# Products of the output half tiles in pairs, and weight half tiles returned inside the second chain

## The chip, the cores and the metric

The kernel runs on one core of a Trainium2 chip. The core has TensorE (PE, with its weight load PEld), VectorE (DVE), ScalarE (ACT), GpSimd (POOL) and SyncE (SP); transfers between the memory (HBM) and the on-chip memory (SBUF) run on 16 DMA engines that all queues share. The metric is the time of one execution in device microseconds, the median of several runs.

## What is computed

Forward and backward of one decoding step of a transformer block, for 2 sequences (B = 2), one new position, 32 heads (64 pairs of sequence and head, called heads below), 8192 cached positions of width 128, all in bf16:

```python
mod = silu(c) @ w_mod                       # sa, ca, ga, sb, cb, gb
h = layernorm(x) * (1 + ca) + sa
scores = einsum('bhqd,bhkd->bhqk', h @ wq, k_cache) * Dh ** -0.5
o = einsum('bhqk,bhkd->bhqd', softmax(scores), v_cache)
x = x + ga * (o @ wo)
h = layernorm(x) * (1 + cb) + sb
out = x + gb * ((silu(h @ w1) * (h @ w3)) @ w2)
# outputs: out, and the gradients of x, k_cache, v_cache, wq, wo, w1, w3, w2, c, w_mod
```

The caches and their gradients hold nearly all of the bytes: per head 2 MB of K and 2 MB of V are read, and 2 MB of dK and 2 MB of dV are written. With the softmax weights p and ds the two gradients are outer products: dV = p (outer) d_o, dK = ds (outer) q.

## The kernel before

**Slots.** The program is written out by a list of events. `at(slot, place, f)` puts a step f into a numbered slot; within a slot the place decides (transposes first, then scores, products for the attention `PL_TT`, returns of buffers `PL_FREE`, products for dK `PL_DK`, single tasks `PL_TASK` last). The loop at the end (L1511 and on) goes through the slots and calls the steps. So each engine gets its instructions in exactly this order and works through them in order, waiting at each for what it needs. A slot has no fixed time.

**The two kinds of head.** An A head (`job_a`) reads K and V: 8 slots of transposes and scores (`a_t`, `a_s`), the softmax, the scaling of K on VectorE (`a_scale`), and products with V (`a_m`). A C head (L1219 and on) reads V again and makes dV and dK: 8 slots of transposes and scores from its slot s (`c_t`, `c_s`), then `c_ds`, and the outer products `c_dv` and `c_dk`. Its transposes are copied out of PSUM by ScalarE or, for two groups of eight in certain stages, VectorE (L383, L385).

**Stages.** Slots 0 to 312: A heads alone, every 8 slots. Slots 312 to about 700: A and C heads take turns, so that each kind comes every 16 slots (the interleaved stage). Slots 704 to 776: C heads alone, every 8 slots, beside them the second of the two chains. From slot 784: C heads alone every 8 slots, with the gradients of the weights put between them, until the last head, number 61, starts at slot 1016.

**The chains.** `steps_chain(b)` (L819) computes for one sequence all that follows the attention: output projection, layernorm, the gated products with w1, w3 and w2, and back. The first runs in the interleaved stage's beginning (slots 272 to 312), the second from slot 721 to 777 (`t1`). Within it, p5 is the last user of w2, p6 follows it; `turn_steps` are the last users of w1 and w3; `end_steps` holds q1, sums and q3.

**Half tiles.** Everything large goes through one pool of 21 buffers of 1 MB, `halfp`: half of a head's K or V, half of a dK or dV, a quarter of wo, pieces of w_mod and wq. w2 takes one, w1 and w3 take three. A count in the program, `free["half"]`, follows them: `release(n)` adds, and `pump` issues the next load of the sorted list `loads` on SP's queue while the count is above `keep` (2 in the interleaved stage, rising from 2 to 8 between slots 785 and 825):

```python
    def pump():
        while loads and free["half"] - keep[0] >= 1:
            loads.pop(0)[2]()
```

The count only sets the order. In the run each load or product into a buffer waits for the buffer's last user: for PE's reading of a K or V tile, or for the landing of an output that was written from it. SP's queue works in order too.

**Products.** `outer` (L1184) makes a quarter of a head's dV or dK (16 of 64 blocks, 128 x 2048) with one VectorE instruction (L1191). The first quarter of each half opens a half tile; after the second an output of 1 MB is issued on POOL's queue (L1196), and the buffer is counted as free six slots later (`back`). c_dv(n, q) is at slot s + 2q. c_dk(n, q) is at s + 11 + 2q, or s + 12 + 2q for the heads in `crow`, nearly all. `c_ds` comes one slot before the first c_dk.

**End of the second chain.** `chain_done` (L1480) at slot t1 drops the weight tiles, counts 4 + 4 half tiles as free (w2 and the three of w1 and w3; four of wo), and takes two for rows of the weight gradients.

Of the kernel before, what the change touches and what calls it, by code (L numbers as in the profile page):

```python
# [17 lines left out]
def kernel(  # L18
# [28 lines left out]
    B, Sq, D = A_x.shape  # L47
    assert Sq == 1 and B == 2
    _, H, Sk, Dh = A_k_cache.shape
# [13 lines left out]
    NG = KK // GRP  # L63
    NQ = KK // QK
    LAG = 2
# [3 lines left out]
    def fsz(fc):  # L69
        return P if fc < FC - 1 else FL  # L70
# [257 lines left out]
    def at(slot, place, f):  # L328
        seq[0] += 1
        events.setdefault(slot, []).append((place, seq[0], f))  # L330

    now = [0]
    PL_EXP, PL_T, PL_X, PL_S, PL_B, PL_MAX, PL_TT, PL_M, PL_FREE, PL_EV, PL_DS, PL_DK, PL_TASK = range(13)
# [8 lines left out]
# [4 lines that stand above are left out]
    def release(n=1):  # L346
        free["half"] += n
# [8 lines left out]
    def scr(n):  # L356
        if cur_ps[0] is None or now[0] - cur_ps[1] > 7:
            head_ps()
        if cur_ps[2] + n > 256:
            cur_ps[2] = 0  # L360
        o = 256 + cur_ps[2]
        cur_ps[2] += n
        return cur_ps[0][:, o:o + n]
# [235 lines left out]
    WH = HN // D  # L599
# [12 lines left out]
    wn = {}  # L612
# [29 lines left out]
    def w2_of(fc):  # L642
        t = wn["w2"][:, fc, :] if fc < WH else w2l[:, fc - WH, :]
        return t[:fsz(fc)]

    def rows_done():
        wn.pop("rows")
        release()
        pump()
# [41 lines left out]
    def small(n, nm, b):  # L691
        return tmp.tile([P, n], F32, name=nm, tag=nm)
# [124 lines left out]
    def steps_chain(b):  # L817
        out = []

        def put(n, f):  # L820
            out.append((n, f))
# [125 lines left out]
            nc.vector.tensor_mul(d_gate_bf[:, :, b], dg[:], dslg[:, :, b])  # L947

        put(1, p6)
        if b == 0:  # L950
            dot_steps(put)
        else:
            turn_steps(put)
# [3 lines left out]
    def dot_steps(put):  # L957
        def rows(v, vec, c0):
            n = min(4, FC - c0)
            ps = tps.tile([P, 4 * P], F32, name="rows", tag="tp")  # L960
            w = 0
            for k in range(n):
                r = fsz(c0 + k)
                nc.tensor.matmul(ps[:, k * P:k * P + r], vec[:r, c0 + k, 0:1].to_broadcast((r, P)),
                                 identb[:r, :r], start=True, stop=True)
                w = k * P + r
            if "rows" not in wn:
                wn["rows"] = hflat()[:]
                free["half"] -= 1
            nc.scalar.copy(wn["rows"][:, v * ROWV + c0 * P:v * ROWV + c0 * P + w], ps[:, 0:w])  # L970

        def one(v, nm, kc, hi):
            w = wn[(nm, hi)][:, kc, :]
            n = w.shape[-1]
            o = v * ROWV + hi * PW
            junk = ktp.tile([P, GRP * P], BF16, name="junkb", tag="kt")
            nc.vector.scalar_tensor_tensor(junk[:, 0:n], w, 1.0, wn["rows"][:, o:o + n], ALU.mult, ALU.mult,
                                           accum_out=dacc[:, kc, 2 * v + hi:2 * v + hi + 1])

        pairs = list(enumerate((("w3", d_up_bf), ("w1", d_gate_bf))))  # L980
        for v, (nm, vec) in pairs:
            for c0 in range(0, FC, 4):
                put(1, lambda v=v, vec=vec, c0=c0: rows(v, vec, c0))
        for v, (nm, vec) in pairs:
            for kc in range(NC):
                put(2, lambda v=v, nm=nm, kc=kc: one(v, nm, kc, 0))
                put(1, lambda v=v, nm=nm, kc=kc: one(v, nm, kc, 1))

    def turn_steps(put):
        b = B - 1  # L990
        groups = []
        for nm, vec in (("w3", d_up_bf), ("w1", d_gate_bf)):
            for f0 in range(0, FC, 2):
                fcs = [f for f in (f0, f0 + 1) if f < FC]
                def mm(kt, vec=vec, fcs=fcs):
                    ps = scr(NC)
                    for dc in range(NC):
                        for n, f in enumerate(fcs):
                            r = fsz(f)
                            nc.tensor.matmul(ps[:, dc:dc + 1], kt[:r, n * NC + dc, :], vec[:r, f, b:b + 1],  # L1000
                                             start=(n == 0), stop=(n == len(fcs) - 1))
                    return ps
                groups.append((nm, fcs, mm))

        def dacc_done(k, ps):
            nc.vector.tensor_copy(dacc[:, :, k], ps)

        turned_steps(put, [(lambda nm=nm, fcs=fcs: [w13_of(nm, kc, f)
                                                    for f in fcs for kc in range(NC)], mm)
                           for nm, fcs, mm in groups], dacc_done)  # L1010

    def end_steps(put, out, b, hold):
        nd = 4 if b == 0 else dacc.shape[-1]

        def sums():
            hold["ps"] = scr(2 * NC)
            nc.tensor.matmul(hold["ps"], onesf[:], hold["both"][:].rearrange("p t k -> p (t k)"),
                             start=True, stop=True)

        def q1():  # L1020
            nc.vector.tensor_reduce(d_h2[:, :, b], dacc[:, :, 0:nd], AX.X, ALU.add)
            both = tmp.tile([P, 2, NC], F32, name="both2", tag="both2", bufs=2)
            nc.vector.scalar_tensor_tensor(both[:, 0, :], mod[:, 4 * NC:5 * NC, b], 1.0, d_h2[:, :, b],
                                           ALU.add, ALU.mult)
            nc.vector.tensor_mul(both[:, 1, :], both[:, 0, :], xn2[:, :, b])
            hold["both"] = both

        def q3():
            st = small(2, "lnst", b)
            nc.vector.tensor_reduce(st[:], hold["ps"].rearrange("p (t k) -> p t k", t=2), AX.X, ALU.add)  # L1030
            nc.vector.tensor_scalar(st[:], st[:], 1.0 / D, None, ALU.mult)
            u = small(NC, "lnu", b)
            nc.vector.tensor_scalar(u[:], xn2[:, :, b], st[:, 1:2], st[:, 0:1], ALU.mult, ALU.add)
            nc.vector.tensor_sub(u[:], hold["both"][:, 0, :], u[:])
            nc.vector.scalar_tensor_tensor(d_x1[:, :, b], u[:], rstd2[:, 0, b:b + 1], dy_col[:, :, b],
                                           ALU.mult, ALU.add)
            nc.vector.tensor_mul(d_attn_bf[:, :, b], mod[:, 2 * NC:3 * NC, b], d_x1[:, :, b])

        put(0, q1)
        put(1, lambda: None)  # L1040
        put(0, sums)
        put(1, q3)
        return out
# [22 lines left out]
    sC = []  # L1066
    s = NG * H
# [10 lines left out]
    s = max(s, TC)  # L1078
# [12 lines left out]
    s = max(s, t1 + 5)  # L1091
# [55 lines left out]
    crow = {n for n in range(NHD) if R0 < sC[n] < A_END - NG or t1 < sC[n]}  # L1147
# [6 lines left out]
    def c_rows(n):  # L1154
        kts[("crow", n)] = rows_out(("c", n))
# [5 lines left out]
    def c_s(n, g):  # L1161
        if n in crow:
            return s_rows(("c", n), n, g, c_bank)
        b, h = hb(n)
        kt = kts.pop(("c", n, g))
        for j in range(GRP):
            cc = g * GRP + j
            nc.tensor.matmul(DP[n][:, cc:cc + 1], kt[:, j, :], DO_bf[:, b, h:h + 1], start=True, stop=True)  # L1168
# [36 lines left out]
    def c_dv(n, q):  # L1205
        outer(dvt, out_3, n, 1, E2[("c", n)], q)
        if q == NQ - 1:
            QD.pop((n, 1))
# [7 lines left out]
    def c_dk(n, q):  # L1216
        outer(dkt, out_2, n, 0, ds2[n], q)
        if q == NQ - 1:
            ds2.pop(n)  # L1219
            QD.pop((n, 0))  # L1220

    for n in range(NHD):
        s = sC[n]
        for g in range(NG):
            at(s + g, PL_T, lambda n=n, g=g: c_t(n, g))
            at(s + g + LAG, PL_S, lambda n=n, g=g: c_s(n, g))
        at(s - 3, PL_B, lambda n=n: c_spread(n))
        for q in range(NQ):
            at(s + 2 * q, PL_TT, lambda n=n, q=q: c_dv(n, q))
            at(s + NG + LAG + 1 + (n in crow) + 2 * q, PL_DK, lambda n=n, q=q: c_dk(n, q))  # L1230
        x = 1 if n in crow else 0
        if x:
            at(s + NG + LAG, PL_EXP, lambda n=n: c_rows(n))
            at(s + NG + LAG + 1, PL_EXP, lambda n=n: c_cols(n))
        at(s + NG + LAG + x, PL_DS, lambda n=n: c_ds(n))

        for hf in range(2):
            if n not in kept:
                want(s + hf * HG, lambda n=n, hf=hf: load_v(("c", n), n, hf))
# [240 lines left out]
    def chain_done():  # L1480
        wn.clear()
        wo_v.clear()
        release(4 + H // WH)
        for k in range(2):
            rowst[k] = hflat()
            free["half"] -= 1
        pump()

    at(t1, PL_TASK, chain_done)

    def more_keep():
# [52 lines left out]
```

## Time and profile before

| | |
|---|---|
| median of 3 runs | 1730.04 us (1729.28 to 1733.95) |
| the profiled execution's own time | 1731.2 us |
| its span | 1729.4 us |
| granted PE clock, mean | 0.83 |
| read from and written to HBM | 421.57 MB, 284.20 MB |
| outputs of 1 MB from half tiles | 256, median 17.9 us from issue to landing |
| loads of V halves | 252, median 14.3 us |
| loads of K halves | 128, median 19.6 us |

The span is that of the instructions on the core; the run's own time is measured around it. Busy times of engines are sums over the whole span. "DMA" is the mean busy share of the 16 DMA engines; packets of one engine overlap a little in the records, so a full stretch reads 1.01. The windows quoted below have, for each stretch, its length, the busy time and the number of instructions of PE, PEld, VectorE, ScalarE and GpSimd, the PE clock, the DMA share and GB/s. A line of waits has: who waited, for whom, the sum in us, how often, and the longest. A line of the timeline has start, length, engine, line and operation, and in brackets the idle time before it and what ended it.

### The profile page before, as it was taken

What the parts mean: (1) busy time and instruction counts of PE and PEld (TensorE: products, weight loads), DVE (VectorE), ACT (ScalarE), POOL (GpSimd) and SP (SyncE); (2) the same over time, 40 slices, a digit from 0 to 9 for tenths busy, and PEclk for the clock granted to TensorE, in tenths of its full rate; (3) what the DMA queues carried; (4) which work ended last, traced back from release to release, by engine and by line L of the source; (5) the groups of instructions that cost most, each with busy time, mean ns of one, the idle gap of its engine ahead of it and who ended that gap; (6) DMA issues with size and microseconds to landing.
All of it is one profiled execution on the core that took longest, in us unless ns stands there. A gap on an engine that the chain in (4) does not pass through costs nothing.

```text
span 1729.4 us, 48571 instructions
## 1 busy us (share of the span) xinstructions
PE 1447.8 (84%) x20883; PEld 1155.6 (67%) x20883; DVE 1149.6 (66%) x1575; ACT 1046.1 (60%) x1536; POOL 344.9 (20%) x726
## 2 busy tenths in 40 slices
PE   5999999989988878887788888975599997797962
PEld 5999998879776666665666666875355565455551
DVE  2666666867877677666667766785586675666554
ACT  4666666646565556555555555697576676566772
POOL 0333333322211111111111112111121111111111
PEclk7999999988999898898888998698765567556586
DMA  9999999999999999999999998999999999999997
GB/s 382 418 418 419 418 419 388 419 387 390 379 412 424 425 425 420 424 418 418 420 419 418 424 419 358 397 416 420 426 411 419 413 410 419 423 420 420 417 420 303
DMA packets 109379, 708.92 MB, mean 410 GB/s; under 512 B 11175, under 2 KB 17683, under 8 KB 27243
## 3 DMA queue, kind: packets, MB, share of 16 engines
q1 hardware_dynamic: 67280, 421.59, 59.4%
q0 software_dynamic: 36864, 268.45, 37.4%
q10 hardware_dynamic: 5019, 15.78, 2.3%
q8 instruction: 163, 2.67, 0.6%
q14 instruction: 53, 0.43, 0.1%
HBM read 421.57 MB, written 284.20 MB: 408 GB/s over the span
## 4 chain that ended last, share of the span: by engine, by line
DMA 45%; PE 35%; DVE 6%; ACT 6%; issue 5%; SPq 1%; POOL 0%; ACTq 0%; POOLq 0%; DVEq 0%
DMA out_dram<-half 24%; DMA half<-in_A_k_cache_dram 16%; PE tp L380 14%; PE m_ps L483 8%; DVE half L1191 4%; DMA out_dram<-stg 3%; ACT kt L385 3%; PE s_ps L442 2%; PE k_ps L505 2%; PE s_ps L433 2%; PE m_ps L413 1%; DMA half<-in_w_mod_dram 1%; PE m_ps L1323 1%; DVE ek L468 1%; PE k_ps L413 1%
## 5 line engine op out<-in xcount | busy, mean ns | idle before, releaser
L385 ACT COPY kt<-tp 128x1024 bf16<-128x1024 bf16 x794 | 796.6, 1017 | 560.0 <-PE tp L380 511.4
L380 PE MATMUL tp<-identb,half 128*128 128x128 bf16 x8192 | 725.3, 243 | 85.8 <-DMA half<-in_A_k_cache_dram 51.2
L380 PEld LDWEIGHTS <-half 128*128 128x128 bf16 x8192 | 579.7, 110 | 212.5 <-issue 149.0
L383 DVE COPY kt<-tp 128x1024 bf16<-128x1024 bf16 x230 | 158.6, 690 | 294.0 <-PE tp L380 291.5
L483 PE MATMUL m_ps<-ek,half 128*128 128x129 bf16 x4096 | 335.6, 225 | 6.9 <-DVE ek L468 3.8
L1196 POOL DMA_DIRECT2D out_dram<-half x256 | 136.2, 532 | 895.2 <-DVE half L1191 734.6
L483 PEld LDWEIGHTS <-half 128*128 128x128 bf16 x4096 | 257.3, 100 | 28.0 <-issue 27.7
L433 PE MATMUL s_ps<-ssel,srow 128*128 128x16 f32 x640 | 98.6, 288 | 49.6 <-ACT srow L420 49.2
L433 PEld LDWEIGHTS s_ps<-ssel,srow 128*128 128x128 f32 x640 | 91.8, 221 | 63.7 <-ACT srow L420 63.4
L442 PE MATMUL s_ps<-qT_bf,kt 128*128 128x1 bf16 x2496 | 107.4, 164 | 0.8 <-DVE lnst L1030 0.4
L442 PEld LDWEIGHTS <-kt 128*128 128x128 bf16 x2496 | 96.6, 97 | 1.3 <-issue 1.0
L1324 ACT CAST stg<-m_ps 128x512 bf16<-128x512 f32 (+2 forms) x124 | 72.8, 588 | 36.0 <-DMA out_dram<-stg 17.6
L1323 PE MATMUL m_ps<-half 2*128 2x512 bf16 (+2 forms) x124 | 70.1, 565 | 12.4 <-DVE d_h_312 L1436 7.3
L505 PE MATMUL k_ps<-half,pz 128*32 128x512 bf16 x1024 | 68.7, 389 | 3.4 <-POOL pz L491 3.2
L454 DVE TENSOR_REDUCE nm<-s_ps 128x1 f32<-128x128 f32 x64 | 18.7, 291 | 36.0 <-PE s_ps L451 35.9
L1168 PE MATMUL s_ps<-DO_bf,kt 128*128 128x1 bf16 x576 | 25.6, 165 | 18.6 <-DVE kt L383 14.5
L505 PEld LDWEIGHTS <-pz 128*32 128x32 bf16 x1024 | 21.6, 97 | 25.1 <-POOL pz L491 5.6
L1168 PEld LDWEIGHTS <-kt 128*128 128x128 bf16 x576 | 24.4, 101 | 19.8 <-DVE kt L383 14.6
L1323 PEld LDWEIGHTS <-half 2*128 2x128 bf16 (+1 forms) x124 | 12.7, 102 | 34.3 <-issue 31.7
L413 PE MATMUL k_ps<-kt,qz_110 128*32 128x512 bf16 x240 | 32.9, 525 | 1.0 <-ACT kt L385 1.0
L413 PE MATMUL k_ps<-kt,qz_109 128*32 128x512 bf16 x240 | 33.3, 535 | 0.0
L1298 ACT CAST half<-m_ps 2x512 bf16<-2x512 f32 (+1 forms) x36 | 20.2, 565 | 20.0 <-PE m_ps L1295 19.4
(899 smaller groups left out, 1996.3 us busy)
## 6 DMA issues: line engine op xcount, KB each, us to landing
out_dram<-half POOLq DMA_DIRECT2D x256, 1024.0 KB, 17.9
half<-in_A_v_cache_dram SPq DMA_DIRECT2D x252, 1024.0 KB, 14.3
half<-in_A_k_cache_dram SPq DMA_DIRECT2D x128, 1024.0 KB, 19.6
out_dram<-stg ACTq DMA_DIRECT2D x22, 512.0 KB, 11.5
half<-in_A_wq_dram SPq DMA_DIRECT2D x8, 1024.0 KB, 13.0
half<-in_A_wo_dram SPq DMA_DIRECT2D x4, 1024.0 KB, 21.6
half<-in_w_mod_dram SPq DMA_DIRECT2D x3, 1024.0 KB, 10.9
half<-in_B_w_dram SPq DMA_DIRECT2D x3, 1024.0 KB
```

Source lines behind the costliest of these rows:

```text
L380: nc.tensor.transpose(tp[:, j, :], block(j), identb[:])
L383: nc.vector.tensor_copy(kt[:], tp[:])
L385: nc.scalar.copy(kt[:], tp[:])
L413: nc.tensor.matmul(R_ps[key][NR * j:NR * (j + 1), :], w, kt[:, o:o + SW, :], start=(a == 0), stop=(a == NSL - 1))
L433: nc.tensor.matmul(sv[:, c, :], t[:, c * P:(c + 1) * P], ssel[:], start=True, stop=True)
L442: nc.tensor.matmul(S_ps[i][:, cc:cc + 1], kt[:, j, :], qT_bf[:, h, b:b + 1], start=True, stop=True)
L483: nc.tensor.matmul(m[:, 0:P + 1], vb_(i, kk), t[:, kk % QK, 0:P + 1], start=(kk == 0), stop=(kk == KK - 1), skip_group_check=True)
L505: nc.tensor.matmul(kp["ps"][NR * j:NR * (j + 1), :], pz[:, o:o + NR], K[(i, kk // HK)][:, kk % HK:kk % HK + QP, :], start=False, stop=(h = ...
L1191: nc.vector.tensor_tensor(pair(t[:, o:o + QK, :]), QD[(n, which)][:].rearrange("p (a b) -> p a b", b=2).unsqueeze(1).to_broadcast((P, QK, ...
L1196: sq_.dma_start(src_of(dst, n)[:, hf * HK:(hf + 1) * HK, :], t[:])
L1323: nc.tensor.matmul(ps[:lw, 0:rw], rsl(ln, lc, lw, step), rsl(rn, rc, rw), start=True, stop=True)
L1324: nc.scalar.copy(st["t"][:lw, o:o + rw], ps[:lw, 0:rw])
```

## The change

The quarter products are put next to each other, two per half tile: c_dv at s + 2, 3, 6, 7 instead of s + 0, 2, 4, 6, and c_dk at s + 12, 13, 16, 17 for all heads, at s + 12, 13, 14, 15 for the last. The half tile of w2 is counted as free right after p6 of the second chain, the three of w1 and w3 before its q1, each with a call of `pump`; `chain_done` then returns the four of wo alone.

```diff
+    def w2_done():
+        wn.pop("w2")
+        release()
+        pump()
+
+    def w13_done():
+        release(3)
+        pump()
+
@@ steps_chain
         put(1, p6)
+        if b == B - 1:
+            put(0, w2_done)
         if b == 0:
             dot_steps(put)
@@ end_steps
+        if b == B - 1:
+            put(0, w13_done)
         put(0, q1)
@@ the C heads
         for q in range(NQ):
-            at(s + 2 * q, PL_TT, lambda n=n, q=q: c_dv(n, q))
-            at(s + NG + LAG + 1 + (n in crow) + 2 * q, PL_DK, lambda n=n, q=q: c_dk(n, q))
+            x, y = 2 + q + q // 2 * 2, NG + LAG + 2 + q + (q // 2 * 2 if s < max(sC) else 0)
+            at(s + x, PL_TT, lambda n=n, q=q: c_dv(n, q))
+            at(s + y, PL_DK, lambda n=n, q=q: c_dk(n, q))
@@ chain_done
-        release(4 + H // WH)
+        release(H // WH)
```

NG is 8, LAG is 2, NQ is 4 and H // WH is 4.

## Prediction

> **What bounds the kernel now.** I read four views, in this order. First the page's row of DMA shares beside the engine rows, to see which resource never rests. Then the table of windows, cut at the places where that row drops, for the price of each drop. Then the waits of the engine that issues the loads and the timeline of VectorE inside the largest drop, for its cause. Last the windows of the end.
>
> ```profile
> PE 1447.8 (84%) x20883; PEld 1155.6 (67%) x20883; DVE 1149.6 (66%) x1575; ACT 1046.1 (60%) x1536; POOL 344.9 (20%) x726
> ...
> DMA  9999999999999999999999998999999999999997
> ```
>
> No computing engine is full, while the mean of the 16 DMA engines is at nine tenths or above in every slice but two: the 25th (1037.8 to 1081.0) and the last. A change to VectorE's order can therefore pay only where DMA engines stand still. The windows size that (the columns after the engines are PE clock, DMA share, GB/s):
>
> ```profile
> 480.00:1060.00 580.00, 478.21 (x6248) 374.13 (x6248) 402.44 (x479) 323.07 (x491) 101.19 (x276) 0.90 1.01 421
> 1060.00:1096.00 36.00, 29.38 (x504) 25.13 (x501) 29.65 (x40) 19.56 (x32) 8.74 (x16) 0.79 0.85 325
> 1096.00:1706.00 610.00, 491.30 (x5098) 344.58 (x5096) 408.33 (x516) 420.39 (x615) 91.75 (x182) 0.68 1.01 418
> 1706.00:1729.40 23.40, 0.00 (x0) 0.00 (x0) 0.09 (x1) 0.00 (x0) 0.53 (x1) 0.50 0.48 201
> ```
>
> A full stretch reads 1.01. The drop at 1060 to 1096 is worth (1.01 - 0.85) x 36 = 5.8 us of an average DMA engine, the tail (1.01 - 0.48) x 23.4 = 12.4 us; the two long stretches have nothing to give. At the drop:
>
> ```profile
> SPq L187 <- DMA out_dram<-half: 56.1, 8, 20.4
> ```
> ```profile
> 1057.72 1.23 DVE L1191 TENSOR_TENSOR half<-Qr,ds_20501 128x2048 bf16<-128x2048 bf16 x1 [2.40 <-DMA out_dram<-half]
> ...
> 1064.78 1.22 DVE L1191 TENSOR_TENSOR half<-Qr,ds_20501 128x2048 bf16<-128x2048 bf16 x1 [2.97 <-PE tp L380]
> ```
>
> The load queue waits once for 20.4 us for an output to leave a half tile; its next load goes out at 1073.95. That output left late because VectorE, which works in order, stopped for 2.40 us and 2.97 us before products whose half tiles were not free. By slots this is 700 to 714, where the last A heads end and C heads come every 8 slots instead of every 16. The free count there falls to -1, no load is issued from slot 700 to 714, and the load at 714 needs the half tile of an output issued at 706.
>
> At the end PE and VectorE are done by 1706.1 and POOL's last five issues each waited for an earlier output:
>
> ```profile
> POOL out_dram L1196 <- DMA out_dram<-half: 9.4, 5, 2.0
> ```
>
> So the tail waits for transfers, not for the last products. Packets in flight confirm it: the number falls from 16 at 1712 to 1 for the last microseconds. One DMA engine ends about 5 us after the next one; the tail is their imbalance.
>
> **What the Trainium skill says.** "Perfetto Trace Analysis", section What "DMA-bound" means, has as its first case specific DMA engines, and that is this kernel: every 1 MB issue is spread over all 16, and the slowest decides. "DMA: Bandwidth & Descriptors", section Why a DMA increments its semaphore by 16 and not by 1, says that a transfer counts as landed only when all participating engines have finished; the tail shows it, and so a half tile comes back at the pace of the slowest engine. Its section Where 436 GB/s comes from gives a ceiling of 435 GB/s; the full stretches show 418 to 421, so no better order will make them faster. "VectorE: DVE Perf Modes", section The perf-mode tier table, has 1224 ns for a bf16 tensor_tensor of 2048 elements; the trace has 1215 to 1228.
>
> **The change part by part.** It adds and removes no computing and no transfer: 256 output DMAs, 512 products of 1.22 us, the same bytes. The instruction counts of all engines stay; only the order moves.
>
> *Pairs.* dV products go from slots s+0, 2, 4, 6 to s+2, 3, 6, 7; dK from s+12, 14, 16, 18 (byrows heads) to s+12, 13, 16, 17, the last head's to s+12 to 15. A half tile is open for 2 slots instead of 3. dV outputs are issued one slot later (s+3, s+7), dK outputs one earlier (s+13, s+17). In a 16-slot period of the interleaved stage the output issues change from slots 2, 2, 6, 14 to 1, 3, 7, 13; the load issues from 8, 8, 10, 11, 12, 12 to 7, 9, 10, 11, 12, 15. All is spread more evenly. Cost in the full stretches: zero, because DMA hides it. The cover: the recurring chain has 20 us from K load to landing and 13 to 15 us from output to landing, while a lone output at 1068.0 had landed when the load behind it went out at 1073.95, 5.9 us later. Two such passes hold 33 - 12 = about 21 us of queueing, to be used up before the period of some 50 us gets longer.
>
> The added wait: in each interleaved period the first dK product now writes into the half tile of the dV output issued 5 slots earlier (before: into one freed by PE). A slot is 50/16 = 3.1 us, so 15.6 us, against a landing of 7.9 to 15.3 us, median 11.4, in this stage. I take zero stall; the upper bound is some 3 us of VectorE in a period, behind which the next kt copies queue, and PE behind them. VectorE is idle for 580 - 402 = 178 us there, 7 us per period, which covers that. If the cover fails, see rival D.
>
> *The drop.* In the changed order the free count stays at 0 or above in slots 700 to 714; the dK half tile opened at 700 comes from a K tile that PE is already done with, and at 704 there is no half tile taken from a V tile just read. Both stalls (2.40 + 2.97 us) should go. Loads come at 711 and 713 instead of 714 and need outputs issued at 701 and 705 instead of 706. But one load that stood at slot 700 is now among those at 711: the drop may begin up to 1 MB / 0.42 = 2.5 us sooner. Bounds for the recovered part: nothing if that load eats it, 5.8 us if all closes. I take 0.6 of it, 3.5 us. What is late next is PE on its V tiles (0.49 us at 1086.94).
>
> *Early return.* w2 comes back at slot 729 and the three of w1/w3 at 742, instead of 777. Four V loads are issued 30 to 48 slots earlier, past nothing but other V loads on SP's queue. The DMA share at 1096 to 1706 is 1.01 already, so their gain is hidden: zero. Their price: products at slots 744 to 760 take half tiles whose output was issued 7 slots before, instead of 11 or more. VectorE may wait there, and the second chain's copies queue behind it; but it waits for a landing, while transfers run. I take zero; bounds -1 (remains of the drop to 1096) and +3 us.
>
> *The end.* The last output can be ready up to three slots earlier, but POOL waited for landings, not for VectorE. Zero; bounds 0 and -2 us (VectorE's last product ended 1.7 us before the last issue).
>
> Sum: -3.5 us on the profiled execution's own 1731.2 us (span 1729.4 and 1.8 around it). On the median of 1730.0, 1.2 below that execution, it gives 1726.5 us.
>
> **Rivals.** *B, the drop closes fully and evener feeding shortens the tail:* -5.8 and 2 of the tail's 12.4: 1722. For it: all four reasons of the drop are touched. Against: the imbalance is a matter of which engine has which packets, and they are the same.
>
> *C, hidden anyway:* the engine that ends last may never have stood still at 1060 to 1096. For it: packets in flight fell there to 1.0 from 1066.5 to 1069 but never to 0. If the same engine is the laggard at the end, the others only wait longer for it: 1730. Against: after 1069 all restart together, and at 1074.5 and 1086 other engines idle too.
>
> *D, slower: the new waits decide.* The place is the first dK product of each interleaved period, waiting on the dV output of 5 slots before. If VectorE stops, the kt copies at g = 2 and 6 wait, PE stops transposing, K half tiles return late and the last K load (already moved from 12 to 15 of the period) follows. For it: in this stage SP waited for outputs nearly all the time, and no product did until now. Against: behind the awaited output stand several loads, so DMA is busy while VectorE waits. The point: with about 24 periods it is slower by over 5.2 us from 0.22 us of DMA idleness each; at 0.5 us each it is 12 us, less the 3.5 won: about 1739.
>
> **How the numbers follow.** A measurement of this kernel can tell about 0.3% from no change, 5.2 us: faster is below 1724.8, slower above 1735.2. Chances: the forecast (1724 to 1729) 0.43, B (1719 to 1724.8) 0.15, C (1729 to 1732) 0.15, D (1734 to 1750, likeliest 1739) 0.27. Faster: B and a fifth of the forecast, 0.24. Slower: nearly all of D, 0.26. The same: 0.50. The range goes from 1720, inside B, to 1739, the middle of D, and leaves out less than 0.2; the likeliest case alone is 1724 to 1729.
>
> **What would show it.** Right: the DMA share of the stretch around 1060 to 1096 at 0.93 or above, no wait of 20 us on SP there and no stop of VectorE before those two products; 1.01 in the long stretches; the tail still some 20 us. Wrong: a product of the half tiles (L1191, L1204 in the changed file) waiting on an output before 1040; a share below 1.00 anywhere between 480 and 1040 or between 1096 and 1700; PE waiting longer for K loads than the 51 us of before; or a total that moves by more than the drop and 2 us together.

## The result, and the profile after

The changed kernel takes 1772.53 us, the median of 4 runs (1767.87 to 1775.71), against 1731.99 us of the kernel before on the same chip (1729.28 to 1734.50): a ratio of 1.0232, interval 1.0202 to 1.0262. It is slower by 40 us, where 1726.5 us with a range from 1720 to 1739 was forecast. The profiled execution, the slowest of the four, has a span of 1773.9 us, 44.5 us more than before.

The page of the changed kernel, its busy row, its row of DMA shares and the row of GB/s under it, in 40 slices:

```profile
PE 1483.4 (84%) x20883; PEld 1189.2 (67%) x20883; DVE 1155.1 (65%) x1575; ACT 1049.1 (59%) x1536; POOL 354.1 (20%) x726
...
DMA  9999999999999999999999999999999999999997
GB/s 383 418 419 418 419 418 391 418 380 396 377 393 386 397 382 400 403 389 392 374 388 386 377 392 378 372 397 424 425 421 416 415 414 418 423 418 415 420 419 314
```

The same row of GB/s on the page of the kernel before:

```profile
GB/s 382 418 418 419 418 419 388 419 387 390 379 412 424 425 425 420 424 418 418 420 419 418 424 419 358 397 416 420 426 411 419 413 410 419 423 420 420 417 420 303
```

The row of shares, on which the prediction rested, shows a kernel that never rests. The row below it shows the loss: from the 12th to the 26th slice the changed kernel moves 372 to 403 GB/s, where the kernel before moves 412 to 425 from its 12th to its 24th, the last ahead of its drop. That is the interleaved stage. The windows of the changed kernel price it (length, then busy us and instructions of PE, PEld, VectorE, ScalarE, GpSimd, then PE clock, DMA share, GB/s):

```profile
480.00:1060.00 580.00, 463.87 (x5764) 364.47 (x5761) 375.71 (x442) 302.16 (x455) 104.74 (x256) 0.85 0.99 390
...
1100.00:1140.00 40.00, 32.82 (x546) 28.15 (x543) 33.00 (x42) 22.42 (x37) 7.55 (x16) 0.95 0.92 346
1140.00:1745.00 605.00, 502.06 (x5171) 357.51 (x5170) 406.33 (x515) 420.80 (x615) 90.01 (x180) 0.66 1.01 417
1745.00:1772.00 27.00, 2.45 (x12) 1.74 (x11) 7.01 (x7) 1.42 (x2) 2.12 (x4) 0.54 0.66 277
```

In the first stretch the rate is 390 GB/s against 421 before, in equal time: (421 - 390) / 421 x 580 = 42.7 us of traffic are missing, about the whole loss. The share fell only from 1.01 to 0.99. The drop has moved to 1100 to 1140 and is still there; the rest runs at 417 GB/s, against 418 before. The PE clock of the first stretch is lower as well, 0.85 against 0.90; an experiment below has 0.85 there without the loss, so the clock is not the cause. The times at which POOL issues its 256 outputs say the same: the first comes 2.3 us later than before, the 89th 47.7 us later, the last 46.2 us later. Between the first and the 89th lie 22 periods (four outputs each), so the loss is 45.4 / 22 = 2.1 us in every period, and in sum nothing after the stage.

Who waits there? Waits of VectorE between 480 and 1040 us, in the kernel before and in the changed one (who, for whom, sum in us, times, longest):

```profile
DVE kt L383 <- PE tp L380: 124.0, 56, 7.4
DVE kt L783 <- PE tp L779: 19.6, 5, 6.0
```
```profile
DVE half L1204 <- DMA out_dram<-half: 88.8, 21, 6.2
DVE kt L383 <- PE tp L380: 74.2, 51, 2.1
```

A wait that didn't exist, of 88.8 / 21 = 4.2 us once per period: a product waits until an output has left its half tile. Waits of PE in the same stretch, before and after:

```profile
PE tp L380 <- DMA half<-in_A_k_cache_dram: 48.8, 27, 4.9
```
```profile
PE tp L380 <- DVE kt L383: 60.8, 25, 4.7
PE k_ps L505 <- POOL pz L491: 21.5, 15, 1.5
```

PE waited for K loads, that is for DMA. Now it waits for VectorE's copies of its transposes (60.8 us), and for small copies on POOL that stand behind an output whose product is late (21.5 us). The second wait weighs little: it is 13.8 and 16.5 us in two runs below that lose nothing. One period in the timeline shows the way. First POOL, then VectorE, then PE in the changed kernel (start, length, engine, line, operation; in brackets the idle time before and what ended it):

```profile
879.08 0.53 POOL L1209 DMA_DIRECT2D out_dram<-half  x1 [5.13 <-DVE half L1204]
```
```profile
884.69 1.22 DVE L468 TENSOR_TENSOR ek<-half,e_17242 128x2048 bf16<-128x2048 bf16 x1
889.46 2.36 DVE L1204 TENSOR_TENSOR half<-Qr,ds_17462 128x2048 bf16<-128x2048 bf16 x2 [3.55 <-DMA out_dram<-half]
891.74 0.68 DVE L383 COPY kt<-tp 128x1024 bf16<-128x1024 bf16 x1
```
```profile
889.90 0.61 PE L380 MATMUL tp<-identb,half 128*128 128x128 bf16 x8
892.47 0.61 PE L380 MATMUL tp<-identb,half 128*128 128x128 bf16 x8 [1.97 <-DVE kt L383]
```

The output issued at 879.08 lands 10.28 us later. VectorE stands still for 3.55 us before the pair of products that writes into its half tile, makes the pair in 2.36 us, and only then copies the transposes (891.74). PE stands still for 1.97 us for that copy. So everything behind it in the period comes later: PE reads K and V half tiles later, and the loads that are to go into them wait for PE. The list for the queue of loads, before and after, shows the last step:

```profile
SPq L187 <- DMA out_dram<-half: 296.0, 44, 13.9
SPq L181 <- DMA out_dram<-half: 194.6, 45, 5.0
```
```profile
SPq L187 <- DMA out_dram<-half: 297.1, 28, 16.3
SPq L181 <- DMA out_dram<-half: 76.5, 20, 6.4
SPq L181 <- PE m_ps L483: 55.6, 21, 3.5
SPq L187 <- PE tp L380: 45.1, 19, 4.2
```

Before, the loads waited for outputs, that is for DMA itself. Now a good 100 us of their waiting are for PE (55.6 for its products with V, 45.1 for its transposes): transfers that are not yet asked for.

Why the half tile changed hands follows from the order in which the program gives them out. In the kernel before, within a period (slots 560 to 575 as the example), the half tile of the output issued at slot 566 goes to the load at 572, and the product at 572 takes a V half tile that PE has read. In the changed kernel the product at 572 takes the half tile of the output issued at 567, and the load, now at 575, takes the V half tile. The two swapped. A load that waits holds up only loads. A product that waits holds up all that VectorE has to do.

### The profile page after: what moved, and what is told of

Same layout as the page of the kernel before. It is cut to its first block, busy times and chain, and to the rows that moved or that the text cites. A ratio compares the mean times of both kernels' runs of the same rounds, so it can differ in the third digit from the quotient of the medians.

```text
span 1773.9 us, 48515 instructions
## 1 busy us (share of the span) xinstructions
PE 1483.4 (84%) x20883; PEld 1189.2 (67%) x20883; DVE 1155.1 (65%) x1575; ACT 1049.1 (59%) x1536; POOL 354.1 (20%) x726
## 4 chain that ended last, share of the span: by engine, by line
DMA 37%; PE 33%; issue 12%; DVE 11%; ACT 4%; POOL 1%; SPq 1%; DVEq 0%; POOLq 0%; ACTq 0%
DMA out_dram<-half 29%; PE tp L380 15%; DVE half L1204 7%; PE m_ps L483 7%; PE s_ps L433 3%; DMA half<-in_A_k_cache_dram 3%; DMA out_dram<-stg 3%; PE s_ps L442 2%; PE k_ps L505 2%; ACT kt L385 2%; PE m_ps L413 2%; DVE ek L468 1%; DMA half<-in_w_mod_dram 1%; DVE kt L383 1%; ACT srow L420 1%
## 5 line engine op out<-in xcount | busy, mean ns | idle before, releaser
L385 ACT COPY kt<-tp 128x1024 bf16<-128x1024 bf16 x794 | 799.7, 1016 | 593.0 <-PE tp L380 549.8
L380 PE MATMUL tp<-identb,half 128*128 128x128 bf16 x8192 | 751.6, 248 | 88.3 <-DVE kt L383 84.5
L380 PEld LDWEIGHTS <-half 128*128 128x128 bf16 x8192 | 605.0, 113 | 214.6 <-issue 209.9
L483 PE MATMUL m_ps<-ek,half 128*128 128x129 bf16 x4096 | 327.0, 222 | 13.8 <-DVE ek L468 10.0
L383 DVE COPY kt<-tp 128x1024 bf16<-128x1024 bf16 x230 | 158.5, 689 | 232.9 <-PE tp L380 232.8
L483 PEld LDWEIGHTS <-half 128*128 128x128 bf16 x4096 | 248.9, 98 | 34.6 <-issue 34.1
L433 PE MATMUL s_ps<-ssel,srow 128*128 128x16 f32 x640 | 115.0, 316 | 43.0 <-ACT srow L420 41.2
L433 PEld LDWEIGHTS s_ps<-ssel,srow 128*128 128x128 f32 x640 | 108.0, 255 | 58.9 <-ACT srow L420 58.8
L505 PEld LDWEIGHTS <-pz 128*32 128x32 bf16 x1024 | 21.6, 96 | 47.7 <-POOL pz L491 28.8
L1424 ACT COPY kt<-tp 128x1024 bf16<-128x1024 bf16 x28 | 29.1, 1041 | 5.4 <-PE tp L1418 3.9
## 6 DMA issues: line engine op xcount, KB each, us to landing
out_dram<-stg ACTq DMA_DIRECT2D x22, 512.0 KB, 10.9
half<-in_w_mod_dram SPq DMA_DIRECT2D x3, 1024.0 KB, 10.9
```

Of the source, the lines that this page charges most:

```text
L380: nc.tensor.transpose(tp[:, j, :], block(j), identb[:])
L383: nc.vector.tensor_copy(kt[:], tp[:])
L385: nc.scalar.copy(kt[:], tp[:])
L433: nc.tensor.matmul(sv[:, c, :], t[:, c * P:(c + 1) * P], ssel[:], start=True, stop=True)
L483: nc.tensor.matmul(m[:, 0:P + 1], vb_(i, kk), t[:, kk % QK, 0:P + 1], start=(kk == 0), stop=(kk == KK - 1), skip_group_check=True)
L505: nc.tensor.matmul(kp["ps"][NR * j:NR * (j + 1), :], pz[:, o:o + NR], K[(i, kk // HK)][:, kk % HK:kk % HK + QP, :], start=False, stop=(h = ...
```

## The experiments

Four theories were to be told apart. W: the place named above, the swap of half tiles and VectorE's wait, through the kt copies. R: the early return of w2, w1 and w3. P: two products in a row (2.36 us instead of 1.22) that hold up the copies by themselves, without a wait. L: the loads moved to later slots of the period, 12 to 15. Each experiment is held against the kernel before on the same chip. Its medians there were 1732.61 us (the first four runs), 1732.01 us (the four runs after them) and 1732.23 us (the last three); the ratios are estimates with their intervals, and differ from the quotient of two medians by up to 0.1%.

**The two halves of the change.** The early return alone, in the changed kernel:

```diff
-            x, y = 2 + q + q // 2 * 2, NG + LAG + 2 + q + (q // 2 * 2 if s < max(sC) else 0)
+            x, y = 2 * q, NG + LAG + 1 + (n in crow) + 2 * q
```

> The early return of w2, w1 and w3 with the products at their old slots. Theory W (the first dK product of each interleaved period waits on the dV output issued five slots before, and VectorE holds PE): that wait is not in this order, so no difference in the interleaved stage, 1724 to 1732 us. Rival R (the early return lets loads take half tiles in front of the products and costs time in and after the second chain): 1735 us or more.

The pairs alone, in the kernel before:

```diff
-            at(s + 2 * q, PL_TT, lambda n=n, q=q: c_dv(n, q))
-            at(s + NG + LAG + 1 + (n in crow) + 2 * q, PL_DK, lambda n=n, q=q: c_dk(n, q))
+            x, y = 2 + q + q // 2 * 2, NG + LAG + 2 + q + (q // 2 * 2 if s < max(sC) else 0)
+            at(s + x, PL_TT, lambda n=n, q=q: c_dv(n, q))
+            at(s + y, PL_DK, lambda n=n, q=q: c_dk(n, q))
```

> The pairs alone, w2, w1 and w3 returned at the end of the chain as before. Theory W: all of the loss is here, 1768 to 1778 us, with some 20 waits of VectorE on outputs between 480 and 1040 us. Rival R: clearly below the 1772 us of the whole change.

The return alone takes 1731.13 us, ratio 0.9997 (0.9987 to 1.0007). The pairs alone take 1772.73 us, ratio 1.0225 (1.0195 to 1.0254), and VectorE's largest wait between 480 and 1040 us is the one of the whole change (the products stand in L1191 here):

```profile
DVE half L1191 <- DMA out_dram<-half: 86.2, 21, 6.3
```

R falls. The loss is in the pairs.

**The pairs of dV and of dK, each alone.** Both in the changed kernel, first the pairs of dV with dK in its old slots, then the pairs of dK with dV in its old slots:

```diff
-            x, y = 2 + q + q // 2 * 2, NG + LAG + 2 + q + (q // 2 * 2 if s < max(sC) else 0)
+            x, y = 2 + q + q // 2 * 2, NG + LAG + 1 + (n in crow) + 2 * q
```

> Only the dV products in pairs, dK products at the slots of before, early return kept. In the built program the first dK product of a period still writes where the dV output issued five slots before it was. Theory W: slow, 1755 to 1778 us, with waits of VectorE on outputs. Rival P (the pairs themselves, 2.4 us of products in a row, hold the copies of transposed blocks up, each of dV and dK with its share): about half of the loss, 1745 to 1755 us.

```diff
-            x, y = 2 + q + q // 2 * 2, NG + LAG + 2 + q + (q // 2 * 2 if s < max(sC) else 0)
+            x, y = 2 * q, NG + LAG + 2 + q + (q // 2 * 2 if s < max(sC) else 0)
```

> Only the dK products in pairs, dV products at the slots of before, early return kept. In the built program the first dK product then writes where PE has freed a V half, and the output's half tile goes to the load queue. Theory W: no loss, 1724 to 1733 us, no wait of VectorE on outputs in the interleaved stage. Rival P: about half of the loss, 1745 to 1755 us.

The dV pairs take 1757.53 us, ratio 1.0135 (1.0106 to 1.0164); the dK pairs 1729.10 us, ratio 0.9983 (0.9976 to 0.9989). VectorE's waits between 480 and 1040 us, first with the dV pairs, then with the dK pairs:

```profile
DVE half L1204 <- DMA out_dram<-half: 99.5, 22, 6.0
DVE kt L383 <- PE tp L380: 72.2, 53, 2.1
```
```profile
DVE kt L383 <- PE tp L380: 116.4, 47, 9.7
```

The dV output that leaves a slot later makes the wait; with the dK pairs alone the half tiles change hands as in the kernel before, and there is no wait. So P falls as the cause: dK pairs cost nothing where nobody waits. They do make the wait dearer. The dV pairs alone have at least as long a wait (99.5 us) as the whole change (88.8 us) and lose 25 us instead of 40. In the timeline above the pair, 2.36 us, stands between the wait and the copy; with single products it is one of 1.22 us. As a count that would be enough for the 15 us between them (24 periods by 1.1 us are 26 us of VectorE), but that it is the reason was not isolated.

**Who takes the half tile.** `KEEP` sets how many half tiles the loads must leave over, so it shifts which user takes which half tile, without moving a product. In the changed kernel first to 3, then to 1, and then to 1 in the kernel before, where it is to make a wait:

```diff
-    KEEP = 2
+    KEEP = 3
```

> The whole change with a reserve of 3 half tiles instead of 2 in the interleaved stage: in the built program the first dK product then writes where PE has read a K half, and the output of five slots before goes to a load. Theory W (the taker of that half tile decides): the loss goes nearly whole, 1725 to 1742 us, no wait of VectorE on outputs there. Rival P (products in a row hold up the copies): still 1765 to 1778 us.

```diff
-    KEEP = 2
+    KEEP = 1
```

> The whole change with a reserve of 1 half tile: here the last K load takes the half tile of the output of five slots before, and the first dK product one that PE has read; one dV product takes one whose output was issued nine slots before (14 us, over the median landing). Theory W: the loss goes, 1725 to 1745 us. Rival P: 1765 to 1778 us. Rival L (the loss is from loads that come late): faster than the change too, but no more than half of the loss, since loads are one half tile ahead.

> The kernel before, products and returns unchanged, with a reserve of 1 half tile: in the built program the second dV half of each interleaved period now writes where the output issued six slots before was (9.4 us of slots against a landing of 11.4 us). Theory W: slower by 5 to 40 us with waits of VectorE on outputs, though no product has moved. Rivals P and L: 1725 to 1732 us, as before or a little better, since loads are further ahead.

With 3 the changed kernel takes 1733.82 us, ratio 1.0002 (0.9992 to 1.0013), and with 1 it takes 1730.09 us, ratio 0.9984 (0.9974 to 0.9994). All products stand where the change put them, and the loss is gone. With 3 no product waits for an output. L falls with the 3: loads are then let out later still, never earlier, and it costs nothing. P falls too, since all pairs are there. VectorE's largest wait with `KEEP` at 3, waits with 1 in the changed kernel, and with 1 in the kernel before:

```profile
DVE kt L383 <- PE tp L380: 130.8, 82, 6.5
```
```profile
DVE half L1204 <- issue: 40.1, 23, 2.3
DVE half L1204 <- PE m_ps L483: 25.1, 23, 1.2
```
```profile
DVE half L1191 <- PE tp L380: 72.9, 22, 3.7
DVE kt L383 <- PE tp L380: 67.2, 56, 2.2
DVE half L1191 <- DMA out_dram<-half: 12.4, 13, 1.7
```

The kernel before gets slower, 1753.43 us, ratio 1.0117 (1.0098 to 1.0136), as W asks for. But its wait isn't the one that was named: the wait for an output is only 12.4 us; 72.9 us are for PE, since the product that opens the second dK half now takes a V half tile that PE is still reading. And PE doesn't wait for the kt copies here, but for a maximum (`rm`) that VectorE makes behind the product. PE's largest wait in this run:

```profile
PE s_ps L451 <- DVE rm L446: 70.9, 22, 3.4
```

That is a loss of the same kind with another last user and another instruction behind the product. "An output has not landed" and "through the kt copies" are not shown by this run. In the changed kernel with 1 VectorE stops as well, 1.1 us per period before one product, for PE (25.1 us in sum), and 1.7 us before another, where the profile shows nothing that it waits for ("issue", 40.1 us). Neither stop costs anything; that they are short and apart may be why, but this was not tested.

**The dK pairs later.** In the changed kernel the dK pairs two slots later in the interleaved stage:

```diff
+            if s < sC[24]:
+                y += 2
```

> The whole change, but in the interleaved stage the dK pairs two slots later (s+14, 15, 18, 19): the K load comes in front of them and takes the half tile of the output of six slots before; the first dK product gets one that PE has read. Theory W: the loss goes, 1725 to 1740 us. Rival P: the pairs are all still there, 1760 to 1778 us.

It takes 1734.11 us, ratio 1.0014 (1.0005 to 1.0022), with no wait on an output in the list. As expected for this run, the K load at slot 573 now stands ahead of the product and takes the half tile of the output; the product gets one that PE has read. So it is again the taker that changed, with all pairs in place. How much time to land would have been enough, this run doesn't tell.

**From VectorE to PE.** The last step of W is that PE suffers through the kt copies. All copies of transposes in slots 328 to 703 were given to ScalarE, in the changed kernel and, as a control, in the kernel before:

```diff
-        if dve:
+        if dve and not 328 <= now[0] < 704:
```

> The changed kernel, with all copies of transposed K and V tiles in slots 328 to 703 made by ScalarE, so that none stands behind VectorE's products. If the loss passes from VectorE's wait to TensorE through these copies (theory W, as rival D told its way), the wait on outputs stays at 60 to 110 us and a part of the 42 us comes back: 1735 to 1760. If the loss passes another way (the output issued later because its product stood waiting, the softmax weights made later), the copies do not matter: 1765 to 1780. ScalarE gets more work, which its control, the kernel before with the same edit, prices.

> The kernel before with the same copies on ScalarE: the price of this edit without any wait on an output. ScalarE is idle for 257 of 580 us in the interleaved stage, so both theories expect 1728 to 1740; what it adds is taken from the reading of the run above.

The changed kernel takes 1736.07 us, ratio 1.0021 (1.0013 to 1.0029), its control 1735.16 us, ratio 1.0017 (1.0008 to 1.0026). The edit takes back practically all of the loss, all but 0.9 us of 40, at the low end of the 1735 to 1760 that W expected. And the wait isn't gone. VectorE's largest wait in the changed kernel with this edit, its window of the stage, and that of the control:

```profile
DVE half L1204 <- DMA out_dram<-half: 161.8, 22, 9.5
```
```profile
480.00:1060.00 580.00, 485.07 (x6240) 377.49 (x6238) 348.92 (x388) 409.89 (x581) 156.75 (x277) 0.85 1.01 414
480.00:1060.00 580.00, 485.06 (x6241) 382.80 (x6238) 355.47 (x386) 408.52 (x585) 165.61 (x278) 0.88 1.01 421
```

VectorE stands still for 161.8 / 22 = 7.4 us per period, nearly twice as long as in the changed kernel; 60 to 110 us were expected. The single waits of the trace say why: VectorE comes to the wait as long after the output's issue as in the changed kernel (a median of 5.9 us against 5.8), but the awaited outputs take longer to land (a median of 13.4 us against 10.6). The transfers run at 414 GB/s; the control's 421 belong to a profiled execution that was 6.8 us shorter, while the medians are 0.9 us apart. PE's list for 480 to 1040 us can no longer have the wait for VectorE's copies (L383); its first line is another one:

```profile
PE m_ps L413 <- POOL qz L1150: 39.6, 18, 3.7
```

So the wait as such costs nothing. What costs is the copy that stands behind it in VectorE's order. The edit also takes some 47 us of work off VectorE (402 us in the kernel before, 355 in the control), which was not separated; but VectorE is busy for only 376 of the 580 us of the changed kernel. The PE clock is 0.85 here, as in the changed kernel.

**A version meant to be faster than both.** The old slots for the interleaved stage, pairs from slot 704 on, and the early return:

```diff
-            x, y = 2 + q + q // 2 * 2, NG + LAG + 2 + q + (q // 2 * 2 if s < max(sC) else 0)
+            x, y = 2 * q, NG + LAG + 1 + (n in crow) + 2 * q
+            if s >= sC[24]:
+                x, y = 2 + q + q // 2 * 2, NG + LAG + 2 + q + (q // 2 * 2 if s < max(sC) else 0)
```

> Old places of the products for all heads of the interleaved stage, pairs from the first head at slot 704, and the early returns. No wait on outputs before slot 704, so the loss of 42 us is gone by theory W. The prediction's gain at the drop, 3.5 us, should then show if it is there: 1723 to 1729. If the drop's gain is eaten by another idle stretch, 1729 to 1733.

It takes 1732.33 us, ratio 1.0001 (0.9994 to 1.0008; 22 runs against 45). The loss is gone and the gain of 3.5 us isn't there. The drop in this kernel:

```profile
1060.00:1096.00 36.00, 25.59 (x373) 21.21 (x373) 27.60 (x35) 17.27 (x28) 6.38 (x15) 0.82 0.83 311
```
```profile
SPq L187 <- DMA out_dram<-half: 47.8, 6, 13.2
SPq L187 <- PE tp L380: 18.5, 2, 12.2
```

The wait of 20.4 us became one of 13.2 us, and another of 12.2 us for PE came in (waits of 1030 to 1110 us). The share is 0.83, against 0.85 before: the drop did not close. Nor did the two stops of VectorE go: before its products it stands still for 4.73 us, for an output, and for 2.28 us, where the kernel before had 2.40 and 2.97.

The two fastest, the dK pairs alone and the changed kernel with `KEEP` at 1, are 0.17% and 0.16% below the kernel before. Both intervals lie under 1, but the differences are smaller than the 0.3% that the prediction took as what can be told from no change.

## Why the prediction was wrong

**The step that failed** is in *Pairs*, "The added wait". The prediction found the right product, the right output and the right distance, 5 slots. It then wrote: "A slot is 50/16 = 3.1 us, so 15.6 us, against a landing of 7.9 to 15.3 us, median 11.4". The length of the slot is wrong by two. The recurring chain comes round every 50 us, but it passes through two periods each time. The stage itself gives the period: from the output issued at 466.2 us to the 96th after it, at 1069.2 us, there are four outputs per period in the kernel before, so 24 periods by 25.1 us. A slot is 25.1 / 16 = 1.6 us, five are 7.8 us, and against the median landing of 11.4 us a wait of 3.6 us follows. The trace has 4.2 us. That these are so near is in part luck: in the changed kernel VectorE comes to the wait a median of 5.8 us after the issue, and the awaited outputs land a median of 10.6 us after it. The text itself could have shown the error: rival D counts about 24 periods, and 24 by 50 us would be 1200 us, twice the stage.

**The cover** that was to hold even then, "VectorE is idle for 580 - 402 = 178 us there, 7 us per period", failed as well. The sum was right (its 7 us are 178 divided by some 24 periods, so here too the period was 25 us), and it was no cover: the idle time lies where VectorE waits for PE's transposes (124.0 us in the kernel before), not between the waiting product and the copy behind it. The run with the copies on ScalarE shows what a cover is: VectorE stands still for 7.4 us per period there, and 0.9 us of the whole time is lost.

**"Cost in the full stretches: zero, because DMA hides it"** holds for the pairs as such (the dK pairs alone 0.9983, `KEEP` at 3 1.0002) and not with the wait. It was read from a share of 1.01.

**The drop.** Both stops of VectorE were to go there, for -3.5 us. In the changed kernel one went and the other became longer, 3.8 us instead of 2.40, and the load queue's wait of 20.4 us is one of 17.7 (1070 to 1150 us):

```profile
DVE half L1204 <- DMA out_dram<-half: 3.8, 1, 3.8
```
```profile
SPq L187 <- DMA out_dram<-half: 63.1, 8, 17.7
```

The share of the drop moved between runs, and the time did not follow: the dK pairs alone have 0.85 there, the changed kernel with `KEEP` at 1 0.90, and both are within 0.2% of the kernel before. By the prediction's own sum, full share less share times length, the drop is worth 5.8 us before, (1.01 - 0.92) x 40 = 3.6 us in the changed kernel and (1.01 - 0.83) x 36 = 6.5 us in the last version. In the last version it changed its place and its cause, as the waits of 13.2 and 12.2 us show. Why the next stop comes in at once, and whether the engine that ends last ever stood still there (rival C), is left open.

**The early return** at zero, bounds -1 and +3: right, 0.9997 alone. **The end** at zero: right to within its bounds; the idle time of an average engine after 1700 us was 12.2 us before and is 10.9 us after 1760 us in the changed kernel.

**Smaller readings.** Five of POOL's last six issues waited for an output, not each of the last five; the products took 1211 to 1260 ns, not 1215 to 1228. Neither bears on the sum. The section of the Trainium skill that the prediction names for a ceiling of 435 GB/s ("DMA: Bandwidth & Descriptors", Where 436 GB/s comes from) gives this as the limit of the SBUF ports, and puts the limit of the HBM side, which it says binds such transfers, at about 358 GB/s. The full stretches here exceed that with 418 to 421 GB/s, so the measurement decides, and the 435 alone does not show that no order could be faster.

**The rivals.** D, at a chance of 0.27, told what happened, with its place and its chain: VectorE stops, the kt copies wait, PE stops, K half tiles come back late. Its price was mis-sized: "at 0.5 us each it is 12 us", and the run has 2.1 us per period. From a wait of 4.2 us half passed through to the period. B did not come: the drop stayed. D's argument against itself, that DMA is busy while VectorE waits, was the error: the rate fell to 390 GB/s, and loads waited for PE. At which moment of a period the queue ran short was not measured. The queue was taken to hold "about 21 us" for a period of 50 us, by the same mistaken period.

**The signs** named in advance: a product waiting on an output before 1040 us came, 21 times. "A share below 1.00 anywhere between 480 and 1040" came with 0.99, a sign so weak that alone it would have been passed over. PE waiting longer for K loads did not come: PE waited for VectorE before it could wait for a load.

## What to carry to other kernels

When a change in order makes buffers change hands in a pool, list for each new user what the buffer's last user was, how long ago it was issued in microseconds (take the period from a count of repeats, not from one turn of a chain) and what stands behind the new user on its engine. A transfer queue may wait for a landing; an engine with the copies that the bounding loop needs may not. Idle time of an engine covers a wait only if it lies between the waiting instruction and the next one that somebody else needs.

## What the runs showed of the hardware

A DMA share near 1 is not a proof that transfers run at full rate. In the stage from 480 to 1060 us the share is 1.01 at 421 GB/s before and 0.99 at 390 GB/s after: 2% less share and 7% less traffic. The packet records between 520 and 1040 us show how: a packet of 8 KB of the loads takes 314.0 ns on average before and 338.6 ns after, and those of 600 ns or more rise from 0.6% to 3.6%. With the copies on ScalarE it is 318.5 ns and 1.2%. So an engine shows as busy while a packet takes longer; what it waits for in that time was not measured. The Trainium skill warns of it in "Perfetto Trace Analysis", section Identifying the Most-Contended Engine: for DMA the HBM utilization is to be used instead of occupancy. This trace agrees, and the prediction, which read the share, did not follow it.

VectorE stands still before its products for 162 of 560 us in one run, and the kernel's time is within 0.9 us of its control; in another it stands still for 89 us, and the kernel loses 40 us. The sum of a wait does not tell its price.
